# Block-sparse attention with a feed-forward network: masks and first weights moved to the front, the other weights paced over two items, V's gathered rows on another queue

## The chip, the cores and the metric

The kernel runs on one core of a Trainium2 chip. The metric is the time of one execution in microseconds (us) on the device. TensorE (PE) multiplies matrices; VectorE (DVE), ScalarE (ACT) and GpSimd (POOL) do elementwise work; SyncE (SP) here only issues DMA transfers. Every engine works through its own list of instructions in order and waits for the others by semaphores. A DMA that an engine issues stands in that engine's list like any other instruction.

## The reference

```python
# q, k, v: (4 sequences, 8 heads, 768 positions, 64); blocks of 32 positions, 24 blocks; 3 sampled blocks per query block
scores = scale * np.matmul(q, k.transpose(0, 1, 3, 2))
mask = np.abs(blk_i - blk_j) <= window                       # window = 1
mask = mask | (blk_i == 0) | (blk_j == 0) | (blk_i == n_blocks - 1) | (blk_j == n_blocks - 1)
for qb in range(n_blocks):
    for kb in sampled_blocks[qb]:
        mask[qb * block:(qb + 1) * block, kb * block:(kb + 1) * block] = True
scores = np.where(mask, scores, -1000000000.0)
attn = softmax(scores)                                       # over the keys
x = np.matmul(attn, v).transpose(0, 2, 1, 3).reshape(3072, 512)
h = x @ w_in                                                 # 512 x 2048
g = np.maximum(0.01 * h, h)
return g @ w_out                                             # 2048 x 512
```

## The kernel before

**Tiles and items.** Twelve tiles of 64 query rows make a sequence. Tile 0 holds the first and the last block, which see all 768 keys; each other tile T has 384 keys: its window, the two end blocks and six sampled blocks. A *unit* is one tile of one pair of heads, so a tile has four units (and tile 0 two parts in each). Four tiles make an *item* of 256 rows; three items make a sequence, twelve the whole. The main loop takes one unit as a step, so the first item is steps 0 to 15, the second 16 to 31, the third 32 to 47.

**Attention of a unit.** Values of 32 bits are split into two 16-bit halves so that TensorE can multiply them. `scores` (L697) multiplies the queries' halves (`qs`, and `qxs` with the halves swapped) by the gathered keys `kg`. The *score pass* `unit_ttr` (L706, on DVE) adds the mask row `em`, scales and takes the minimum; `unit_exp` (L718, ACT) takes the exponential and its sum; `pair_norm` gives `r`, the reciprocal of the sum. In the first item alone, TensorE turns the probabilities: `unit_high` (L738) builds a diagonal matrix of `r` from an identity (`eye32`), `unit_turn` (L756) multiplies by it and splits the result into `pt`. In later items ACT and DVE split the probabilities (`pp`, L745 and L766) and a DMA transposes them into `pt` (L771). `pair_av` (L798) multiplies V's rows by `pt`.

**Gathering.** `gather_k` copies a tile's keys from `kt` into one of two buffers `kg`, the sampled blocks on POOL (L640), at addresses that POOL reads from `offs`. V's halves are written to `scr` in memory (L496); `gather_v` loads a tile's rows from there into one of two buffers `vg`: the window (L659) and, when a buffer is new to a sequence, the two end blocks (L663) on SP's queue, the sampled blocks with an indirect DMA on POOL (L666).

**Masks.** `build_masks` makes `offs`, the table `mask` and `eye32`: small DVE instructions, one POOL instruction (L272) and a matmul of TensorE (L281). It is called in step 1 and set behind a score pass by `behind`, which adds an ordering edge.

**Feed-forward.** For each finished item `ffn_h` (L833) multiplies by w_in, `ffn_act1`, `ffn_max` and `ffn_act2` apply the nonlinearity and split, `ffn_o` (L860) multiplies by w_out. The weights come in four quarters. The first two items take the quarters one at a time as they get ready, later items all at once.

**Weights.** `prep_weights` is a generator. A quarter has one part of w_in and one of w_out; a part is loaded in groups of 1 MB (the last two parts in groups of 0.5 MB). The loads are issued on SP (L344); the weights come as 64-bit numbers, and each group is *decoded* to 32 bits (L351 on ACT, L352, L353 and L355 on DVE), a finished part is squared and summed (`squares`, L197 on TensorE) for its scale, and split into halves (L414 on ACT, L419 on DVE). The main loop advances the generator by credits: the table `"wr"` says from which step on how many credits a step gives. Decoding a group of 1 MB costs four.

**What sets the order.** The code gives each instruction a priority; a scheduler places them on the engines' lists. Edges added by `behind` fix an order where the code asks for it.

Of the kernel before, what the change touches and what calls it, by code (L numbers as in the profile page):

```python
# [15 lines left out]
AF = mybir.ActivationFunctionType  # L16
# [44 lines left out]
    "wlate": 1200,  # L61
    "wr": [(0, 1.8), (16, 3.5)],
    "wsplit": "dddddddd",
# [5 lines left out]
def tile_block_sparse_attention_ffn(  # L69
# [151 lines left out]
    def latest():  # L221
        return nc.cur_bb.bb.instructions[-1].name
# [140 lines left out]
    def prep_weights():  # L363
# [33 lines left out]
        behind(begin, last_sp["q"])  # L397
        yield 1
        invs = {}

# [165 lines left out]
    def prep_q(b, j, i, rq):  # L566
# [16 lines left out]
        nc.sync.dma_start_transpose(out=qs, in_=flat(qa))  # L583
        last_sp["q"] = latest()
        qxs = pa.tile([P, H, P], F16, tag="qxs", name=f"qxs_{nm}", bufs=2)
        nc.sync.dma_start(out=qxs[:D], in_=qs[D:])
        nc.sync.dma_start(out=qxs[D:], in_=qs[:D])
        qstack[b, j, i] = (qs, qxs, inv)
        yield 0.8
# [64 lines left out]
    def gather_v(b, T):  # L654
# [3 lines left out]
        t0 = (T - 1) * Q2  # L658
        nc.sync.dma_start(out=vg[:, 0, :], in_=scr[b][t0:t0 + P, :])  # L659
        if vends.get(n) != b:  # L660
            vends[n] = b
            for i, at in enumerate((0, S - BLOCK)):
                nc.sync.dma_start(  # L663
                    out=vg[Q2 + i * BLOCK:Q2 + (i + 1) * BLOCK, 2, :], in_=scr[b][at:at + BLOCK, :])
# [67 lines left out]
    def unit_high(u):  # L732
        u.r = u.pair.r[:, u.pi:u.pi + 1]
        if u.item.n < CFG["pe_t"]:
            if u.parts == 2 or u.pi == 0:
                u.pair.pp = pa.tile([P, 2, 2, KEYS], F16, tag="pp", name=f"pp_{u.nm}", bufs=CFG["pp"])
            u.diag = u.pair.pp.rearrange("p a l t -> p (a l t)").bitcast(F32)[:, u.pi * P:(u.pi + 1) * P]
            nc.gpsimd.tensor_scalar(out=u.diag, in0=eye32, scalar1=u.r, scalar2=None, op0=ALU.mult)  # L738
            return
# [320 lines left out]
    for hp in range(NP):  # L1060
        load_v(0, hp)
    begin = len(nc.cur_bb.bb.instructions)
    load_rows()
    behind(begin + 1, last_sp["k", NP - 1])
    start(("v", 0), prep_v(0))

# [48 lines left out]
    for u in units:  # L1115
        it, ui = u.item, u.k * NP + u.hp
        b, nb = it.b, it.b + 1

        if step == 1:
            begin = len(nc.cur_bb.bb.instructions)  # L1120
            build_masks()
            behind(begin, last_ttr[0])
        if step == 2:
# [32 lines left out]
        for w in CFG["ord"]:  # L1156
# [50 lines left out]
            elif w == "w":  # L1207
# [5 lines left out]
                while wcredit >= 1.0:  # L1213
                    c = next(weights, "end")
                    wcredit -= c if c != "end" else wcredit
                if step < 16:
                    behind(begin, last_ttr[0])
# [72 lines left out]
```

## Time and profile before

| | |
|---|---|
| median of three runs | 869.46 us (865.9 to 872.94) |
| the profiled execution | 867.32 us, its span 865.6 us, mean granted TensorE clock 0.963 |
| TensorE busy | 745.7 us, 86% of the span |
| VectorE busy | 601.8 us, 70% |
| ScalarE busy | 509.9 us, 59% |
| GpSimd busy | 356.3 us, 41% |
| DMA | 135.33 MB, mean 156 GB/s |

The profile is of one execution. A row of a group names the line, the engine, the operation, the output and the inputs by the program's names, and the shapes; then the count, the busy time and the mean of one in nanoseconds, and behind the second bar the idle time just before them with what ended it. A row of a stretch gives the busy time (and the number of instructions) of PE, PE's weight loads, DVE, ACT and POOL, the granted clock, the DMA engines' share and their GB/s. Durations of neighbours on one engine can overlap at their ends, so a group's busy time is less than its count times its mean.

### The profile page before, as it was taken

What the parts mean: (1) busy time and instruction counts of PE and PEld (TensorE: products, weight loads), DVE (VectorE), ACT (ScalarE), POOL (GpSimd) and SP (SyncE); (2) the same over time, 40 slices, a digit from 0 to 9 for tenths busy, and PEclk for the clock granted to TensorE, in tenths of its full rate; (3) what the DMA queues carried; (4) which work ended last, traced back from release to release, by engine and by line L of the source; (5) the groups of instructions that cost most, each with busy time, mean ns of one, the idle gap of its engine ahead of it and who ended that gap; (6) DMA issues with size and microseconds to landing.
All of it is one profiled execution on the core that took longest, in us unless ns stands there. A gap on an engine that the chain in (4) does not pass through costs nothing.

```text
span 865.6 us, 20081 instructions
## 1 busy us (share of the span) xinstructions
PE 745.7 (86%) x7140; PEld 494.9 (57%) x7140; DVE 601.8 (70%) x1595; ACT 509.9 (59%) x1183; POOL 356.3 (41%) x473
## 2 busy tenths in 40 slices
PE   1456667766998899998999989999999999999997
PEld 1245545443756565665666566666666666666674
DVE  4668998988968678757966777778667676663221
ACT  4556676775634667666656757667467566553211
POOL 0416744642125346345543554453434554532121
PEclk9968979887999999999999999999999999999999
DMA  9877489998648879898759899967678576566000
GB/s 205 162 225 237 160 191 230 234 216 181 137 104 145 172 163 211 160 170 147 194 124 177 159 162 203 199 133 183 144 131 175 116 158 148 120 139 86 26 2 25
DMA packets 312771, 135.33 MB, mean 156 GB/s; under 512 B 279773, under 2 KB 292062, under 8 KB 312670
## 3 DMA queue, kind: packets, MB, share of 16 engines
q1 hardware_dynamic: 307038, 116.74, 64.9%
q0 software_dynamic: 5632, 17.31, 8.2%
q8 instruction: 56, 0.92, 0.5%
q14 instruction: 45, 0.37, 0.1%
HBM read 65.58 MB, written 12.58 MB: 90 GB/s over the span
## 4 chain that ended last, share of the span: by engine, by line
PE 43%; DVE 20%; DMA 18%; ACT 8%; issue 5%; SPq 3%; POOL 1%; POOLq 1%; ACTq 0%; DVEq 0%
PE o L860 17%; PE h L833 17%; PE av L798 4%; PE s L697 4%; DMA kt<-k_k 3%; DVE pp L766 3%; ACT p L718 3%; DVE p L706 3%; DMA rq<-in_q_dram 3%; DMA qs_q<-qa_q 3%; DMA qxs_q<-qs_q 2%; DMA pt<-pp 2%; DMA wbuf<-in_moe_w_out_dram 2%; DVE ht L842 1%; DMA rk<-in_k_dram 1%
## 5 line engine op out<-in xcount | busy, mean ns | idle before, releaser
L860 PE MATMUL o<-W,g 128*128 128x512 f16 x1152 | 273.8, 383 | 9.3 <-DVE g L846 6.7
L833 PE MATMUL h<-x,W 128*128 128x256 f16 x2304 | 276.0, 277 | 1.9 <-ACT ht L839 1.9
L833 PEld LDWEIGHTS <-W 128*128 128x128 f16 x2304 | 223.9, 100 | 49.0 <-issue 14.2
L847 POOL TENSOR_TENSOR g<-ht,g 128x512 f16<-128x512 f32 x96 | 116.4, 1213 | 312.7 <-DVE g L846 279.1
L860 PEld LDWEIGHTS <-g 128*128 128x128 f16 x1152 | 108.2, 98 | 132.4 <-issue 15.0
L718 ACT ACTIVATE p<-p,mx 128x384 f32<-128x384 f32 x208 | 126.1, 607 | 98.0 <-DVE mx L706 66.7
L640 POOL COPY kg<-kt 128x256 f16 x264 | 133.1, 531 | 76.6 <-PE s L697 42.6
L766 DVE SCALAR_TENSOR_TENSOR pp<-p,r,pp 128x384 f16<-128x384 f32 x188 | 125.3, 694 | 33.1 <-ACT pp L745 32.4
L666 POOL DMA_INDIRECT vg<-scr,rows x88 | 94.2, 1071 | 69.5 <-PE av L798 47.4
L842 DVE SCALAR_TENSOR_TENSOR ht<-ht 128x512 f32<-128x512 f32 x96 | 67.8, 706 | 75.2 <-ACT ht L839 75.0
L706 DVE CUSTOM_DVE_ANT_0 p<-s,em,nsc 128x384 f32<-128x384 f32 x176 | 102.9, 610 | 21.9 <-PE s L697 17.3
L745 ACT ACTIVATE pp<-p,r 128x384 f16<-128x384 f32 x188 | 104.1, 604 | 17.1 <-DVE r L730 15.6
L798 PE MATMUL av<-pt,vg 128*64 128x128 f16 x2112 | 80.8, 225 | 19.7 <-DMA pt<-pp 13.6
L798 PEld LDWEIGHTS <-vg 128*64 128x64 f16 x2112 | 68.3, 112 | 49.1 <-issue 43.9
L839 ACT ACTIVATE ht<-h,gd 128x512 f32<-128x512 f32 x80 | 54.1, 677 | 63.9 <-PE h L833 51.0
L697 PE MATMUL s<-kg,qs_q 128*64 128x384 f16 x352 | 60.7, 343 | 21.5 <-DVE mx L706 21.2
L697 PE MATMUL s<-kg,qxs_q 128*64 128x384 f16 x352 | 60.0, 336 | 6.1 <-DMA qxs_q<-qs_q 6.1
L697 PEld LDWEIGHTS <-qs_q 128*64 128x64 f16 x416 | 26.9, 110 | 55.5 <-issue 43.5
L846 DVE CAST g<-ht 128x512 f16<-128x512 f32 x96 | 42.3, 441 | 10.3 <-PE o L860 8.3
L730 DVE RECIPROCAL r<-sum 128x2 f32<-128x2 f32 x96 | 15.4, 160 | 36.3 <-ACT sum L729 35.6
L718 ACT ACTIVATION_READ_ACCUMULATOR p<-p,mx 128x1 f32 x208 | 39.1, 188 | 0.0
L571 ACT ACTIVATE qa_q<-rq 128x512 f16<-128x512 f32 x25 | 15.7, 628 | 38.8 <-DMA rq<-in_q_dram 38.8
(136 smaller groups left out, 762.1 us busy)
## 6 DMA issues: line engine op xcount, KB each, us to landing
vg<-scr SPq DMA_DIRECT2D x44, 256.0 KB, 3.8
qxs_q<-qs_q SPq DMA_DIRECT2D x48, 128.0 KB, 2.6
v<-in_v_dram SPq DMA_DIRECT2D x32, 192.0 KB, 4.8
scr<-v SPq DMA_DIRECT2D x16, 384.0 KB, 4.7
W<-in_moe_w_in_dram SPq DMA_DIRECT2D x5, 1024.0 KB, 9.4
rq<-in_q_dram SPq DMA_DIRECT2D x20, 256.0 KB, 6.1
out_dram<-ob SPq DMA_DIRECT2D x20, 256.0 KB, 3.1
rk<-in_k_dram SPq DMA_DIRECT2D x24, 192.0 KB, 4.7
```

The source lines that it names most:

```text
L640: nc.gpsimd.tensor_copy(out=kg[:, :, slot * BLOCK:(slot + 1) * BLOCK], in_=kt[:, :, bass.ds(off, BLOCK)])
L666: nc.gpsimd.indirect_dma_start(out=vg[:n_, c, :], out_offset=None, in_=scr[b][:, :], in_offset=bass.IndirectOffsetOnAxis(ap=rows[:n_, c - ...
L697: nc.tensor.matmul(o, a, k, start=(n == 0), stop=(n == 1)))
L706: nc.vector.tensor_tensor_reduce(out=u.p[i], in0=u.sp[i], in1=kgs[u.b, u.T][1] if u.T else zero.to_broadcast([P, KEYS]), scale=u.nsc, scal ...
L718: nc.scalar.activation(u.p[i], u.p[i], AF.Exp, scale=-1.0, bias=u.mx[:, :1], accum_out=u.pair.sum[:, u.pi, i:i + 1])
L745: nc.scalar.activation(pp[:, 0, :], p, AF.Copy, scale=u.r)
L766: nc.vector.scalar_tensor_tensor(out=pp[:, 1, :], in0=p, scalar=u.r, in1=pp[:, 0, :], op0=ALU.mult, op1=ALU.subtract)
L798: nc.tensor.matmul(o, a, m, start=(c == 0 and l == 0), stop=(c == n - 1 and l == 1)))
L833: nc.tensor.matmul(c.ph[:, i], w, x, start=(d == 0 and m == 0), stop=(d == NP - 1 and m == 2)))
L842: nc.vector.scalar_tensor_tensor(out=c.t, in0=c.t, scalar=0.01, in1=c.t, op0=ALU.mult, op1=ALU.max)
L847: nc.gpsimd.tensor_tensor(out=c.g[:, 1], in0=c.t, in1=c.g[:, 0], op=ALU.subtract)
L860: nc.tensor.matmul(o, a, w, start=(c.first and i == 0 and m == 0), stop=(c.last and i == 1 and m == 2)))
```

## The change

Six edits:

1. `build_masks` is called ahead of the main loop, right behind the row loads, and no longer in step 1 behind a score pass.
2. The generator of the weights is advanced once more ahead of the main loop, and a new stage in it lets four groups be loaded instead of two, behind the last transpose of the first sequence's keys. The second group is ordered behind the second half of the `qxs` copies instead of the `qs` transpose.
3. From step 16 on a step gives 1.7 credits instead of 3.5, and from step 32 on 4.5. (Ahead of step 16 it stays at 1.8.)
4. For the first sequence V's window and end rows are loaded from GpSimd's queue instead of SP's.
5. The diagonal matrix is made on ScalarE instead of GpSimd.
6. In step 0 the weights' instructions are no longer ordered behind a score pass.

```diff
-    "wr": [(0, 1.8), (16, 3.5)],
+    "wr": [(0, 1.8), (16, 1.7), (32, 4.5)],
...
         load(2)
         behind(begin, last_sp["q"])
+        yield 1
+        begin = len(nc.cur_bb.bb.instructions)
+        load(4)
+        behind(begin, last_sp["k", NP - 1])
...
         nc.sync.dma_start_transpose(out=qs, in_=flat(qa))
-        last_sp["q"] = latest()
         qxs = pa.tile([P, H, P], F16, tag="qxs", name=f"qxs_{nm}", bufs=2)
         nc.sync.dma_start(out=qxs[:D], in_=qs[D:])
         nc.sync.dma_start(out=qxs[D:], in_=qs[:D])
+        last_sp["q"] = latest()
...
-        nc.sync.dma_start(out=vg[:, 0, :], in_=scr[b][t0:t0 + P, :])
+        queue = nc.sync if b else nc.gpsimd
+        queue.dma_start(out=vg[:, 0, :], in_=scr[b][t0:t0 + P, :])
...
-                nc.sync.dma_start(
+                queue.dma_start(
                     out=vg[Q2 + i * BLOCK:Q2 + (i + 1) * BLOCK, 2, :], in_=scr[b][at:at + BLOCK, :])
...
-            nc.gpsimd.tensor_scalar(out=u.diag, in0=eye32, scalar1=u.r, scalar2=None, op0=ALU.mult)
+            nc.scalar.activation(u.diag, eye32, AF.Copy, scale=u.r)
...
+    next(weights)
     begin = len(nc.cur_bb.bb.instructions)
     load_rows()
     behind(begin + 1, last_sp["k", NP - 1])
+    build_masks()
     start(("v", 0), prep_v(0))
...
-        if step == 1:
-            begin = len(nc.cur_bb.bb.instructions)
-            build_masks()
-            behind(begin, last_ttr[0])
...
-                if step < 16:
+                if 0 < step < 16:
                     behind(begin, last_ttr[0])
```

The order of the instructions on the engines moves with it. In the names below the digits behind `p`, `pp`, `s` and `pt` are the item in its sequence, the tile in the item, the pair of heads and, for score passes, the part; the last number is a buffer's. Line numbers of the changed program are a few higher than before.

ScalarE, from the first unit's exponential on, before:

```order
L718 ACTIVATE p_0_0_0_0_240,sum_0_0_0_246<-p_0_0_0_0_240,mx_0_0_0_242 128x384
L718 ACTIVATE p_0_0_0_1_241,sum_0_0_0_246<-p_0_0_0_1_241,mx_0_0_0_242 128x384
L571 ACTIVATE qa_q_0_1_262,ss_q_0_1_261<-rq_0_1_207 128x512
L571 ACTIVATE qa_q_0_1_375,ss_q_0_1_374<-rq_0_1_207 128x512
L718 ACTIVATE p_0_0_1_0_311,sum_0_0_0_246<-p_0_0_1_0_311,mx_0_0_1_313 128x384
L718 ACTIVATE p_0_0_1_1_312,sum_0_0_0_246<-p_0_0_1_1_312,mx_0_0_1_313 128x384
L476 ACTIVATE v_0_0_265,ssv_264<-v_0_209 128x768
L476 ACTIVATE v_0_0_265,ssv_264<-v_1_212 128x768
L476 ACTIVATE v_0_0_265,ssv_264<-v_2_215 128x768
L476 ACTIVATE v_0_0_265,ssv_264<-v_3_218 128x768
L645 ACTIVATE em_1_466<-mask 128x384
L645 ACTIVATE em_2_715<-mask 128x384
```

and now:

```order
L723 ACTIVATE p_0_0_0_0_281,sum_0_0_0_287<-p_0_0_0_0_281,mx_0_0_0_283 128x384
L723 ACTIVATE p_0_0_0_1_282,sum_0_0_0_287<-p_0_0_0_1_282,mx_0_0_0_283 128x384
L649 ACTIVATE em_1_466<-mask 128x384
L649 ACTIVATE em_2_715<-mask 128x384
L723 ACTIVATE p_0_0_1_0_312,sum_0_0_0_287<-p_0_0_1_0_312,mx_0_0_1_314 128x384
L723 ACTIVATE p_0_0_1_1_313,sum_0_0_0_287<-p_0_0_1_1_313,mx_0_0_1_314 128x384
L743 ACTIVATE pp_0_0_0_337<-eye_88,r_0_0_0_334 128x128
L743 ACTIVATE pp_0_0_1_358<-eye_88,r_0_0_0_334 128x128
L575 ACTIVATE qa_q_0_1_303,ss_q_0_1_302<-rq_0_1_207 128x512
L575 ACTIVATE qa_q_0_1_376,ss_q_0_1_375<-rq_0_1_207 128x512
L764 ACTIVATE pt_0_0_0_339<-turn_0_0_0_340 128x384
L480 ACTIVATE v_0_0_306,ssv_305<-v_0_209 128x768
```

The mask rows `em` and the diagonals `pp` stand ahead of the next queries' squares (`qa`), where all four of V's squares and those of the queries stood ahead of the mask rows; the diagonals were not on this engine.

SyncE, behind the load of V, before:

```order
L241 DMA rows<-in_sampled_blocks_dram 32x11x1 x6
L344 DMA W<-in_moe_w_out_dram 128x2x1024
L583 DMA_TRANSPOSE qs_q_0_1_517<-qa_q_0_1_375 128x8x128
L516 DMA rq_1_0_668<-in_q_dram 128x8x64
L496 DMA scr_564<-v_0_0_265 128x6x256
L344 DMA W<-in_moe_w_out_dram 128x2x1024
L586 DMA qxs_q_0_1_519<-qs_q_0_1_517 64x1024
L587 DMA qxs_q_0_1_519<-qs_q_0_1_517 64x1024
L496 DMA scr_564<-v_0_1_569 128x6x256
L496 DMA scr_564<-v_0_2_646 128x6x256
L496 DMA scr_564<-v_0_3_729 128x6x256
```

and now:

```order
L344 DMA W<-in_moe_w_out_dram 128x2x1024 x2
L241 DMA rows<-in_sampled_blocks_dram 32x11x1 x6
L587 DMA_TRANSPOSE qs_q_0_1_517<-qa_q_0_1_376 128x8x128
L520 DMA rq_1_0_668<-in_q_dram 128x8x64
L344 DMA W<-in_moe_w_in_dram 128x2x1024
L500 DMA scr_564<-v_0_0_306 128x6x256
L589 DMA qxs_q_0_1_519<-qs_q_0_1_517 64x1024
L590 DMA qxs_q_0_1_519<-qs_q_0_1_517 64x1024
L500 DMA scr_564<-v_0_1_569 128x6x256
L344 DMA W<-in_moe_w_out_dram 128x2x1024
L500 DMA scr_564<-v_0_2_646 128x6x256
```

Both groups of the first w_out part stand ahead of the sampled rows and the query transpose, and two more weight loads stand among the writes of V to `scr`.

VectorE, around the probability splits of the last tile of sequence one, before:

```order
L154 RECIPROCAL v_s<-v_inv 128x1
L873 TENSOR_TENSOR beta_all<-top,v_inv 128x1
L730 RECIPROCAL r_2_3_2_3760<-sum_2_3_2_3639 128x2
L492 SCALAR_TENSOR_TENSOR v_1_0_2829<-v_0_2151,v_s,v_1_0_2829 128x6x64 x2
L842 SCALAR_TENSOR_TENSOR ht_1_0_3228<-ht_1_0_3228 128x512
L766 SCALAR_TENSOR_TENSOR pp_2_3_2_3763<-p_2_3_2_0_3631,r_2_3_2_3760,pp_2_3_2_3763 128x384
L766 SCALAR_TENSOR_TENSOR pp_2_3_2_3763<-p_2_3_3_0_3671,r_2_3_2_3760,pp_2_3_2_3763 128x384
L846 CAST g_1_0_3231<-ht_1_0_3228 128x512
L881 SCALAR_TENSOR_TENSOR ob_0_0_2115<-o_0_12_0_3146,beta_3_3273,ob_0_0_2115 128x512
L492 SCALAR_TENSOR_TENSOR v_1_1_3626<-v_1_2326,v_s,v_1_1_3626 128x6x64 x2
L881 SCALAR_TENSOR_TENSOR ob_0_1_2117<-o_0_12_1_3147,beta_3_3273,ob_0_1_2117 128x512
```

and now:

```order
L771 SCALAR_TENSOR_TENSOR pp_2_3_0_3566<-p_2_3_0_0_3445,r_2_3_0_3557,pp_2_3_0_3566 128x384
L771 SCALAR_TENSOR_TENSOR pp_2_3_0_3566<-p_2_3_1_0_3487,r_2_3_0_3557,pp_2_3_0_3566 128x384
L423 SCALAR_TENSOR_TENSOR W<-W,wi_s 128x512 x3
L142 TENSOR_REDUCE v_tot<-v_sum 128x1
L423 SCALAR_TENSOR_TENSOR W<-W,wi_s 128x512
L847 SCALAR_TENSOR_TENSOR ht_1_0_3075<-ht_1_0_3075 128x512
L143 TENSOR_SCALAR v_tot<-v_tot 128x1
L771 SCALAR_TENSOR_TENSOR pp_2_3_2_3712<-p_2_3_2_0_3560,r_2_3_2_3709,pp_2_3_2_3712 128x384
L771 SCALAR_TENSOR_TENSOR pp_2_3_2_3712<-p_2_3_3_0_3620,r_2_3_2_3709,pp_2_3_2_3712 128x384
L851 CAST g_1_0_3078<-ht_1_0_3075 128x512
L147 TENSOR_SCALAR v_ex<-v_tot 128x1
L352 TENSOR_SCALAR W<-W 128x512 x3
```

Where V's splits for sequence two and the output of the last quarter stood, the splits of the last w_in part and the decodes of the last w_out part stand now.

## The prediction

> **What bounds the kernel now.** I read the busy time by stage first. The stages are cut where VectorE starts the first score pass (L706) of a tile: 60.6 us is the first tile of the sampled kind, 165.6 us the first tile of the third item, 214.7 us the last tile of sequence one, 318.6 us the fifth tile of sequence two.
>
> ```profile
> core 0: us, PE busy (x) PEld busy (x) DVE busy (x) ACT busy (x) POOL busy (x), PEclk, DMA share, GB/s
> 0.00:27.00 27.00, 4.63 (x18) 3.07 (x19) 9.19 (x39) 10.79 (x17) 0.82 (x6) 1.00 1.06 216
> 27.00:60.60 33.60, 16.00 (x119) 12.14 (x119) 23.92 (x89) 18.74 (x42) 11.18 (x19) 0.85 0.80 195
> 60.60:165.60 105.00, 74.19 (x805) 55.85 (x804) 97.38 (x233) 72.68 (x159) 58.12 (x72) 0.87 0.80 206
> 165.60:214.70 49.10, 31.94 (x305) 18.34 (x303) 42.83 (x115) 35.26 (x84) 19.23 (x23) 0.86 0.98 201
> 214.70:318.60 103.90, 94.93 (x883) 63.06 (x882) 78.69 (x217) 59.76 (x137) 35.06 (x50) 0.99 0.73 149
> 318.60:865.60 547.00, 524.02 (x5019) 342.44 (x5016) 349.80 (x907) 312.68 (x746) 231.89 (x305) 0.99 0.69 139
> ```
>
> The same windows for L706 alone confirm the cuts: each pass is two instructions (the pass and the read of its minimum), a tile of this kind has four, so 56 rows are seven tiles, 24 are three, 48 are the last tile, the first tile of sequence two (eight passes) and three more.
>
> ```profile
> 60.60:165.60 105.00, 17.14 (x56) 0.87 0.80 206
> 165.60:214.70 49.10, 7.15 (x24) 0.86 0.98 201
> 214.70:318.60 103.90, 14.26 (x48) 0.99 0.73 149
> ```
>
> VectorE (DVE) is the bound from 60.6 to 165.6 us (idle 7.6 of 105.0 us) and nearly so to 214.7 us (idle 6.3). From there TensorE (PE) is: idle 9.0 of 103.9 us, then 23.0 of 547.0. The first 60.6 us are bound by neither: DVE idle 17.8 + 9.7, PE idle 22.4 + 17.6. So a gain can come only from idle time ahead of 60.6 us and from moving work between a stretch where DVE is full and one where it is not.
>
> The timeline shows what the first 60 us wait for, engine by engine (start, length, and in brackets the idle time before it).
>
> ```profile
> 26.49 0.62 DVE L706 CUSTOM_DVE_ANT_0 p<-s,zero,nsc 128x384 f32<-128x384 f32 x1 [7.14 <-PE s L697]
> 29.53 1.21 POOL L640 COPY kg<-kt 128x256 f16 x3 [12.18 <-DVE hit L266]
> 36.73 0.15 DVE L730 RECIPROCAL r<-sum 128x2 f32<-128x2 f32 x1
> 37.43 0.43 POOL L272 TENSOR_SCALAR_AFFINE_SELECT at<-ok 24x66 f32<-24x66 f32 x1
> 37.86 1.19 POOL L738 TENSOR_SCALAR pp<-eye,r 128x128 f32<-128x128 f32 x2
> 37.91 1.06 PE L281 MATMUL mask_ps<-at,tmps 24*128 24x33 f32 x4 [5.93 <-POOL at L272]
> 39.77 2.91 PE L756 MATMUL turn<-pp,p 128*128 128x128 f32 x12
> 60.67 0.62 DVE L706 CUSTOM_DVE_ANT_0 p<-s,em,nsc 128x384 f32<-128x384 f32 x1 [2.45 <-PE turn L756]
> ```
>
> The masks are computed after the first pass; TensorE, stuck in order at the mask's matmul, turns nothing until 39.77 us, though r is there at 36.73. Behind that, ScalarE (ACT) waits in order for a query load that it does not need yet, and DVE for ACT; and from 37.5 to 46.5 us the DMA engines move 6 GB/s at a share of 0.12.
>
> ```profile
> ACT qa_q L571 <- DMA rq<-in_q_dram: 6.5, 2, 5.7
> DVE v L492 <- ACT v L489: 4.3, 2, 3.7
> 37.50:46.50 9.00, 7.76 (x40) 6.33 (x41) 6.80 (x24) 7.58 (x16) 1.90 (x4) 1.00 0.12 6
> ```
>
> **The change part by part.** Prices of single instructions:
>
> ```profile
> L738 POOL TENSOR_SCALAR pp<-eye,r 128x128 f32<-128x128 f32 x16 | 12.5, 788 | 17.4 <-DVE r L730 17.3
> L729 ACT ACTIVATE sum<-sum,floor 128x2 f32<-128x2 f32 x88 | 25.1, 286 | 0.7
> L805 ACT ACTIVATE avt<-av 128x256 f32<-128x256 f32 x48 | 17.7, 368 | 16.3 <-PE av L798 16.0
> L492 DVE SCALAR_TENSOR_TENSOR v<-v,v_s,v 128x384 f16<-128x384 f32 x32 | 21.9, 724 | 6.0 <-ACT v L489 6.0
> L353 DVE SCALAR_TENSOR_TENSOR W<-W 128x1024 int32<-128x1024 int32 x9 | 11.3, 1258 | 0.0
> L355 DVE SCALAR_TENSOR_TENSOR W<-W 128x1024 int32<-128x1024 int32 x9 | 11.1, 1230 | 0.0
> L352 DVE TENSOR_SCALAR W<-W 128x1024 int32<-128x1024 int32 x12 | 8.7, 723 | 3.5 <-ACT W L351 3.5
> L353 DVE SCALAR_TENSOR_TENSOR W<-wbuf,W 128x512 int32<-128x512 int32 x8 | 6.2, 790 | 0.0
> L355 DVE SCALAR_TENSOR_TENSOR W<-wbuf,W 128x512 int32<-128x512 int32 x8 | 5.3, 683 | 0.0
> L352 DVE TENSOR_SCALAR W<-W 128x512 int32<-128x512 int32 x8 | 3.9, 499 | 0.9 <-ACT W L351 0.9
> L419 DVE SCALAR_TENSOR_TENSOR W<-W,wi_s 128x1024 f16<-128x1024 f32 x6 | 7.9, 1322 | 0.0
> L554 DVE SCALAR_TENSOR_TENSOR k_k<-rk,k_s,k_k 128x768 f16<-128x768 f32 x12 | 12.1, 1011 | 2.4 <-ACT k_k L552 2.4
> L766 DVE SCALAR_TENSOR_TENSOR pp<-p,r,pp 128x384 f16<-128x384 f32 x188 | 125.3, 694 | 33.1 <-ACT pp L745 32.4
> L666 POOL DMA_INDIRECT vg<-scr,rows x22: 899/1062/1943, 62.9 to 208.2; - x22
> L659 SPq DMA_DIRECT2D vg<-scr x12: 338/368/572, 62.0 to 261.8; - x12
> ```
>
> *Masks and the first decode early; the diagonal on ScalarE.* The mask arithmetic and one weight decode (0.72 + 1.26 + 1.23 = 3.2 us) now stand ahead of the first pass, inside DVE's 7.14 us wait at 26.49; that pass keeps its time, and about 5 us of DVE work (the decode and some 2 us of small mask rows) leave the 10.2 us between it and r. So r comes at about 31.5 instead of 36.73. The diagonal takes two instructions on ACT, priced between 0.286 and 0.368 us; I take 0.33, nearer the wider row, so sixteen cost ACT 5.3 us (4.6 to 5.9), covered by ACT's 32 us of idle time from 60.6 to 165.6; were half of it bare, it would cost 2.6. The turn then starts at about 32.5, where it was 39.77.
>
> From the turn to the first sampled pass lie 20.9 us. Eight V splits (L492, 8 x 0.72 = 5.8 us) now stand behind that pass, and DVE's longest wait on ACT (3.7 us) goes, since the next item's query squares move behind it on ACT: 20.9 - 5.8 - 3.7 = 11.4, so 44. I allow 2.5 for the longer work now ahead of it on ACT: **46.5 instead of 60.7**. Of the 14.2 us, 5.8 are work that is still owed, so **8.4 us of idle time are saved**; bounds 3 (a query load that still lands late) to 11.
>
> *Weights in items one and two (1.8 a step kept, then 1.7 for 3.5).* Counting both orders on DVE up to the third item's first pass, the new one lacks one decode of the large form (3.2), three of the half form but for one L355 (3 x 0.50 + 3 x 0.79 + 2 x 0.68 = 5.2), two splits of W (2.6) and small rows (1.7), and has a K split (1.0), two probability splits (1.4) and scale rows (1.0) more: 9.3 us less. Neighbours overlap at their ends, so I count 8.6 us. DVE is full there, so this comes off the time. All in all the third item starts 8.4 + 8.6 = 17 us earlier.
>
> *Two megabytes of w_out ahead of the query transpose on SP.* They are queued at about 35 us and fall into those 9 us; a third load now stands ahead of the first V write, a fourth ahead of the third. At the 201 to 206 GB/s of the stages a 1 MB load takes 5 us; what V's write loses, the earlier split must give back. I allow **4 us** of new waits (0 to 10) before the third item: the net gain there is 13.
>
> *V's rows on GpSimd.* Eleven tiles' rows and four ends leave SP for POOL. Where SP took 0.37 us for one, POOL takes about what an indirect one takes: 15 x 1.06 = 16 us (5.5 to 29), for 12.5 us of diagonals that left, against 46.9 us that POOL idles from 60.6 to 165.6. The first tile has five issues before its V is whole where it had two: 3 us later, hidden because TensorE's V product of that tile now stands behind the scores of the tile two on. At 0 in the sum. [...]
>
> *The third item gives part back (4.5 a step).* For TensorE the unit prices are
>
> ```profile
> 188.63 2.64 PE h L833 x24
> 415.65 2.59 PE o L860 x12
> 315.69 0.86 PE L798 MATMUL av<-pt,vg 128*64 128x128 f16 x24 [0.94 <-DVE xf L808]
> 173.89 10.34 DMA pt<-pp
> ```
>
> From 165.6 to the last tile's first pass DVE has another 22.6 - 9.3 = 13.3 us less (weights, and FFN that waits for them); overlap off, 12.4: that stage is 36.7 instead of 49.1 us. What was not done then comes in the next stage: by the order TensorE has two blocks of h (2 x 2.64), 24 matmuls of o (24 x 0.216), 72 of av (3 x 0.86) and 28 of the weights' squares (at one to two av matmuls each, 1 to 2 us) more: 15 us. That stage is TensorE's: 94.9 + 15 + 9.0 idle = 119 instead of 103.9. DVE, with 78.7 + 21, stays below. Net **+2.7**.
>
> *After 318.6 us* both orders have done the same on DVE and TensorE, and ACT has only the sixteen diagonals behind it: 547.0 us unchanged.
>
> **Sum.** 8.4 + 8.6 - 4 - 2.7 = 10.3 us off the span of 865.6 us: 855.3. The profiled execution took 867.3 us, 1.7 us outside its span, and lies 2.1 below the median of 869.46; I take the 10.3 us off the median: **859 us**.
>
> **The rivals.**
> *More than that, 848 us:* no new waits (4), the sampled pass at 44 (2.5), and in the third item DVE loses the waits that fill its 6.3 us of idle time, as the 10.34 us of a probability transpose in the chain at 173.89. For it: the DMA share of 0.98 there is made of weights that now load sooner. Against: the half-size loads still go there, at 4.5 a step.
>
> *GpSimd's queue takes it back, 867 us:* at 1.94 us each the ten issues for the first two tiles take 19 us where POOL had six of four indirect ones; tile one's V comes 8 us late (half of the 13 more, and the two ends), and TensorE, in order, stands at its product with DVE behind it: 859 + 8. Against: POOL idles nearly half that stage. [...]
>
> *The weights ahead of V on SP, 868 us:* two extra megabytes stand in front of the last V write, 10 us at 201 GB/s. If the first product of a sampled tile is due before V's rows, the 10 show but for the 1 us by which the order puts that product later: 859 + 9. Against: the 9 us at 6 GB/s, which hold 1.8 MB.
>
> *Slower, 880 us:* the last quarter decides. Its eight half-size loads and decodes now stand around the last tile, in order on DVE in front of V's splits for sequence two, and on TensorE its squares stand ahead of the scale of sequence two's first query. If a load comes behind a probability transpose of 10.34 us, everything of sequence two stands behind it; two such waits cost 21 us: 859 + 21. It decides where the loads of the third item (some 3 MB beside 3 MB of K and V and the transposes) need more than the stage's 36.7 us. For it: the DMA share of 0.98 in that stage before. Against: 0.73 in the next one, into which half of it falls.
>
> **How the numbers follow.** Forecast 859 (own range 853 to 864) 0.43; 848 0.17; 867 0.12; 868 0.13; 880 0.15. About 1% (8.7 us: 860.8 and 878.2) is what a measurement of this kernel can tell from no change. Faster by that: all of the 0.17, and three quarters of the forecast's own range lie below 860.8, 0.33: 0.50. Slower: 0.12 of the 880 case. The rest, 0.38, is within. The range 845 to 876 leaves out 0.14 of the 880 case and 0.04 below the 848.
>
> **What would show it.** In the changed profile: the first pass that reads em at 46.5 us (44 to 50) instead of 60.67, and the turn near 32.5; the third item's first pass near 153; the last tile of sequence one near 189; the fifth tile of sequence two near 308; 547 us from there. The forecast is wrong if the third item starts after 160, if GpSimd's direct issues take well over 1.1 us with TensorE waiting for vg, or if DVE waits at L352 for a load of the last quarter while TensorE stands at a wo square.

## The result, and the profile after

| | before | changed |
|---|---|---|
| median | 865.37 us (20 runs, 859.0 to 872.94) | 862.85 us (20 runs, 855.7 to 867.16) |
| ratio | 1 | 0.9947, 95% interval 0.9925 to 0.9968 |
| profiled execution | 867.32 us, span 865.6 | 863.27 us, span 861.6 |
| mean granted clock of the profiled execution | 0.963 | 0.948 |

The ratio is worth 4.6 us (2.8 to 6.5), in the profiled pair 4.0 us; the two medians lie 2.5 us apart. Ratios and median clocks, here and below, leave out the few runs that took over 1.5% more than the fastest of their kernel. The forecast was a gain of 10.3 us. That the 859 us forecast lies so near 862.85 is luck in part: it was taken off a median of 869.46, and more runs of the kernel before have one of 865.37, from which the same gain would have given 855.

The windows of the changed kernel, cut at the same passes as before (now L711): the first tile of the sampled kind, the first tile of the third item, the last tile of sequence one, the fifth tile of sequence two.

```profile
core 0: us, PE busy (x) PEld busy (x) DVE busy (x) ACT busy (x) POOL busy (x), PEclk, DMA share, GB/s
0.00:44.00 44.00, 18.57 (x90) 13.00 (x91) 28.80 (x120) 26.92 (x58) 6.60 (x19) 0.98 0.99 228
44.00:151.00 107.00, 74.65 (x768) 54.70 (x769) 94.20 (x230) 75.69 (x174) 53.18 (x71) 0.75 0.87 201
151.00:186.70 35.70, 25.10 (x246) 15.58 (x240) 33.95 (x84) 28.11 (x68) 15.49 (x20) 0.86 1.06 253
186.70:309.10 122.40, 109.87 (x1024) 72.32 (x1022) 98.33 (x260) 69.23 (x154) 45.13 (x58) 0.96 0.74 152
309.10:861.60 552.50, 525.34 (x5029) 344.13 (x5026) 342.80 (x907) 312.47 (x746) 233.11 (x305) 0.99 0.69 138
```

| start of | before | forecast | changed | gain |
|---|---|---|---|---|
| first sampled pass | 60.6 | 46.5 | 44.0 | 16.6 |
| third item | 165.6 | 153 | 151.0 | 14.6 |
| last tile of sequence one | 214.7 | 189 | 186.7 | 28.0 |
| fifth tile of sequence two | 318.6 | 308 | 309.1 | 9.5 |
| end of span | 865.6 | 855.3 | 861.6 | 4.0 |

So each stage of the forecast is found within 2.5 us down to 309 us, and then 5.5 us are lost in a stretch that was to stay as it was. But VectorE's passes are not TensorE's time, and in that region TensorE is the bound (busy 525.3 of 552.5 us). The timelines of TensorE have the first scores of the fifth tile of sequence two, of the kernel before and of the changed one:

```profile
313.91 0.35 PE L697 MATMUL s<-kg,qs_q 128*64 128x384 f16 x2
```

```profile
306.62 0.35 PE L702 MATMUL s<-kg,qs_q 128*64 128x384 f16 x2
```

On TensorE the gain there is 7.3 us; VectorE's pass merely follows sooner (2.5 us behind instead of 4.7). So 3 us of the 10.3 are missing at this point and 3.3 more at the end.

The timeline of the changed kernel's early part: r, the diagonal on ScalarE, the turn, and the first sampled pass.

```profile
29.12 0.16 DVE L735 RECIPROCAL r<-sum 128x2 f32<-128x2 f32 x1
29.37 0.69 ACT L743 ACTIVATE pp<-eye,r 128x128 f32<-128x128 f32 x2 [1.00 <-DVE r L735]
44.00 0.62 DVE L711 CUSTOM_DVE_ANT_0 p<-s,em,nsc 128x384 f32<-128x384 f32 x1 [0.83 <-PE turn L761]
```

And the groups of the changed kernel for what was moved: V's rows on GpSimd, the indirect gathers, the diagonal on ScalarE.

```profile
L664 POOL DMA_DIRECT2D vg<-scr x11 | 6.8, 614 | 52.0 <-PE av L803 41.3 <-DMA scr<-v 10.6
L668 POOL DMA_DIRECT2D vg<-scr x4 | 2.1, 541 | 0.0
L671 POOL DMA_INDIRECT vg<-scr,rows x88 | 93.9, 1067 | 46.7 <-issue 18.3 <-PE av L803 12.1 <-DMA scr<-v 11.7
L743 ACT ACTIVATE pp<-eye,r 128x128 f32<-128x128 f32 x16 | 5.5, 392 | 1.5 <-DVE r L735 1.0 <-DVE W L352 0.4
```

**TensorE works longer for the same matmuls.** Its busy time was 745.7 us; the five rows above add up to 753.5, for 7140 matmuls in both. The difference is the clock: by the mean granted clock, (1 - 0.963) x 865.6 x 2 = 64 us at half speed before and (1 - 0.948) x 861.6 x 2 = 90 us after. Both figures leave out the start. The clock's records begin at 43.5 us before and at 35.5 us in the changed kernel, and the profile counts the time ahead of them as full speed (the 1.00 in the first rows); but the score matmuls there take 0.53 us, as at 45.17 us of the changed kernel at a clock of 0.50, and 0.33 to 0.35 behind at 1.00 (a turn of six matmuls 1.65 us at 33.68 us and 0.94 at 35.83). With the whole start counted at half speed, an estimate from these times, it is 108 us before and 124 after. TensorE is busy for 60 and 79 us of these, and half of the 19 us between is 9, by that estimate about the 7.8 by which its busy time grew.

In both traces the clock is recorded as 0.50 or 1.00. The changed kernel from 93.56 us on, cut every 3.41 us (columns as above; the last three are the clock, the DMA share and GB/s):

```profile
93.56:96.98 3.42, 3.42 (x34) 2.96 (x33) 3.42 (x8) 1.92 (x6) 3.42 (x5) 0.50 0.20 71
96.98:100.39 3.41, 0.98 (x10) 0.50 (x9) 3.41 (x15) 2.86 (x6) 1.24 (x2) 1.00 0.01 2
100.39:103.80 3.41, 1.50 (x26) 1.30 (x24) 3.41 (x7) 3.01 (x7) 1.73 (x2) 0.50 0.19 23
103.80:107.21 3.41, 1.15 (x7) 0.54 (x7) 3.41 (x10) 1.58 (x3) 1.83 (x2) 0.50 1.01 214
107.21:110.63 3.42, 2.00 (x29) 1.31 (x26) 3.27 (x5) 3.31 (x8) 2.73 (x3) 0.50 1.13 199
110.63:114.04 3.41, 3.41 (x18) 2.27 (x17) 3.41 (x10) 2.04 (x5) 2.07 (x4) 0.50 0.61 125
114.04:117.45 3.41, 3.41 (x33) 3.04 (x31) 2.16 (x6) 2.98 (x9) 0.00 (x0) 1.00 1.24 191
```

TensorE is busy 0.98 us of one such window, and the clock of the next is 0.50; it is 1.00 again behind a window in which TensorE is busy throughout (3.41 us). Behind the start, and but for one at the very end, the 24 stretches at half clock in the two traces last 3.4, 6.8, 10.2, 13.7 or 17.1 us, all whole multiples of 3.41 us. In these two traces each of the 19 windows of that length at full clock in which TensorE was busy for less than 1.4 us was followed by half clock, and none with more than 2.0 us was; back at full it was only behind windows with 2.7 us or more. Among 35 runs of the kernel before the granted clock lies at a median of 0.955, among the 20 of the changed one at 0.946. In the 23 runs that the first experiments had of the kernel before, each per cent of clock goes with 4.3 us of time; in the 28 and the 34 of the two later sets it is 3.0 and 2.6 us.

### The profile page after: what moved, and what is told of

Its sections match the earlier page's. It is cut to its first block, busy times and chain, and to the rows that moved or that the text cites. A ratio compares the mean times of both kernels' runs of the same rounds, so it can differ in the third digit from the quotient of the medians.

```text
span 861.6 us, 20081 instructions
## 1 busy us (share of the span) xinstructions
PE 753.5 (87%) x7140; PEld 499.7 (58%) x7140; DVE 598.1 (69%) x1595; ACT 512.4 (59%) x1199; POOL 353.5 (41%) x472
## 4 chain that ended last, share of the span: by engine, by line
PE 52%; DMA 19%; DVE 16%; ACT 6%; issue 4%; SPq 2%; POOLq 0%; POOL 0%; ACTq 0%; DVEq 0%
PE h L838 20%; PE o L865 19%; PE av L803 5%; DMA qs_q<-qa_q 5%; PE s L702 5%; DMA pt<-pp 4%; DVE pp L771 3%; DMA qxs_q<-qs_q 3%; DMA kt<-k_k 3%; DVE p L711 2%; ACT p L723 2%; DMA wbuf<-in_moe_w_out_dram 2%; DVE W L353 2%; DMA v<-in_v_dram 1%; PE turn L761 1%
## 5 line engine op out<-in xcount | busy, mean ns | idle before, releaser
L711 DVE CUSTOM_DVE_ANT_0 p<-s,em,nsc 128x384 f32<-128x384 f32 x176 | 102.5, 610 | 24.8 <-PE s L702 20.2
L671 POOL DMA_INDIRECT vg<-scr,rows x88 | 93.9, 1067 | 46.7 <-issue 18.3
L803 PE MATMUL av<-pt,vg 128*64 128x128 f16 x2112 | 83.0, 229 | 17.5 <-DVE top L448 7.8
L803 PEld LDWEIGHTS <-vg 128*64 128x64 f16 x2112 | 70.4, 115 | 46.2 <-issue 39.5
L702 PE MATMUL s<-kg,qs_q 128*64 128x384 f16 x352 | 62.6, 348 | 23.8 <-DVE mx L711 20.7
```

The source lines that it names most:

```text
L671: nc.gpsimd.indirect_dma_start(out=vg[:n_, c, :], out_offset=None, in_=scr[b][:, :], in_offset=bass.IndirectOffsetOnAxis(ap=rows[:n_, c - ...
L702: nc.tensor.matmul(o, a, k, start=(n == 0), stop=(n == 1)))
L711: nc.vector.tensor_tensor_reduce(out=u.p[i], in0=u.sp[i], in1=kgs[u.b, u.T][1] if u.T else zero.to_broadcast([P, KEYS]), scale=u.nsc, scal ...
L803: nc.tensor.matmul(o, a, m, start=(c == 0 and l == 0), stop=(c == n - 1 and l == 1)))
```

## The experiments

All ratios are to the kernel before on the same chip; 0.001 is 0.87 us. One thing holds for every kernel here: the scheduler places the instructions anew, so a run that undoes one part also has another order. Between the changed kernel and the one that only moves V's rows back to SyncE, the lists of TensorE's 7140 matmuls in order of time show 600 lines of difference.

| kernel | ratio (95%) | median clock |
|---|---|---|
| changed | 0.9947 (0.9925 to 0.9968) | 0.946 |
| old rate, the rest changed | 0.9922 (0.9892 to 0.9953) | 0.950 |
| new rate alone | 1.0077 (1.0041 to 1.0112) | 0.944 |
| rate 1.8, 2.5, 4.5 | 1.0086 (1.0052 to 1.0121) | 0.938 |
| rate 1.8, 5.0 | 1.0019 (0.9983 to 1.0054) | 0.944 |
| rate 2.5, 3.5 | 0.9956 (0.9925 to 0.9988) | 0.949 |
| V's rows on SyncE | 1.0041 (1.0008 to 1.0074) | 0.941 |
| the same, without 2 MB ahead | 1.0005 (0.9981 to 1.0030) | 0.943 |
| diagonal on GpSimd | 1.0101 (1.0064 to 1.0137) | 0.943 |
| both of these undone | 1.0032 (1.0001 to 1.0063) | 0.949 |
| masks late | 1.0015 (0.9981 to 1.0049) | 0.946 |
| two extra pairs | 1.0119 (1.0068 to 1.0170) | 0.948 |
| four extra pairs | 1.0098 (1.0057 to 1.0139) | 0.958 |

### The rate of the weights

*The old rate in the changed kernel.*

```diff
-    "wr": [(0, 1.8), (16, 1.7), (32, 4.5)],
+    "wr": [(0, 1.8), (16, 3.5)],
```

> The changed kernel with the weights' old rate (1.8 a step, from step 16 on 3.5); masks, V's rows and the diagonal stay as changed. Theory one, the last quarter: what is missing from the forecast went where the last quarter now stands, at 4.5 a step around the last tile of sequence one. Then the third item starts some 8 us later than in the changed kernel (TensorE's first scores near 158 instead of 150.0 us), but the stage from the last tile of sequence one to the fifth tile of sequence two falls from 126 to some 110 us, the fifth tile starts at 302 to 305 instead of 306.6, and the time is 2 to 5 us under the changed kernel's. Rival, the clock: TensorE's 7.8 us of extra busy time for the same matmuls come from the early work being packed differently, whichever rate is used; then TensorE's busy time up to the fifth tile stays above 222 us (218.3 before, 226.1 changed) and the time stays within 2 us of the changed kernel's. The prediction's own sum: the rate is worth 8.6 - 2.7 and about 4 of new waits, so undoing it costs some 2 us.

0.9922: 2 us under the changed kernel by the two ratios, though their intervals overlap. Its windows at the same cuts:

```profile
42.70:161.10 118.40, 82.18 (x813) 59.10 (x813) 104.98 (x244) 80.03 (x179) 54.28 (x72) 0.78 0.82 203
161.10:212.10 51.00, 35.59 (x359) 22.69 (x358) 44.50 (x117) 34.45 (x82) 23.48 (x28) 0.83 0.92 188
212.10:310.60 98.50, 90.58 (x843) 59.75 (x842) 78.63 (x213) 59.46 (x137) 35.12 (x50) 0.98 0.81 156
```

This pair differs by the rate alone, and shows it as a loan. With the new rate the stretch to the third item is 11.4 us shorter and the third item 15.3 us (51.0 to 35.7), for VectorE has 10.8 and 10.6 us less to do. But TensorE also does 7.5 and 10.5 us less there, and 19.3 us more in the next stretch, which is its own: that one is 23.9 us longer (98.5 to 122.4). Of 26.7 us, 23.9 are paid back by the fifth tile of sequence two. The first theory's place is right, but its gain of 2 to 5 us is not shown by the ratio's interval, and the fifth tile does not start earlier (its first scores at 309.5 us, not 302 to 305). The clock rival's sign holds: TensorE is busy 224.7 us up to there, above 222, so in the changed kernel the longer matmuls are there at either rate.

*The new rate alone*, with all else as before:

```diff
-    "wr": [(0, 1.8), (16, 3.5)],
+    "wr": [(0, 1.8), (16, 1.7), (32, 4.5)],
```

> The kernel before with the new rate of the weights alone (1.8 a step, from step 16 on 1.7, from step 32 on 4.5); no other part of the change. The prediction's sum for the rate: 8.6 us less VectorE work ahead of the third item, 2.7 given back, so some 2 to 6 us faster than before. What undoing the rate in the changed kernel showed speaks for no gain: there the time fell by some 2 us (859.5) rather than rising, so the rate alone should be 0 to 3 us slower than before. If the halved clock comes from the rate, the mean clock falls from 0.958 to below 0.950; if it comes from the early start, it stays at 0.955 to 0.965.

1.0077, so 6.7 us (3.6 to 9.7) slower than before, worse than either expectation, with the clock at 0.944. Its windows:

```profile
58.90:165.90 107.00, 74.74 (x712) 52.07 (x712) 89.34 (x221) 71.54 (x161) 55.28 (x72) 0.76 0.81 190
165.90:203.90 38.00, 27.45 (x299) 17.65 (x299) 35.00 (x93) 28.34 (x66) 12.72 (x18) 0.82 1.03 251
203.90:320.40 116.50, 107.30 (x991) 71.62 (x987) 95.33 (x251) 67.87 (x152) 41.33 (x54) 0.97 0.71 146
```

VectorE has 8.0 us less to do ahead of the third item (97.38 to 89.34; the forecast said 8.6), and the stretch is 2 us longer: VectorE now idles 17.7 of 107.0 us, where it idled 7.6 of 105.0, and the granted clock there is 0.76 instead of 0.87.

*Three other rates.* Each is the changed kernel with another table.

```diff
-    "wr": [(0, 1.8), (16, 1.7), (32, 4.5)],
+    "wr": [(0, 1.8), (16, 2.5), (32, 4.5)],
```

> The changed kernel with a rate between the two: 1.8 a step, from step 16 on 2.5, from step 32 on 4.5. If the lower rate beside the second and third item is what costs TensorE its clock (mean clock 0.944 for the new rate alone against 0.956 for the kernel before, and 6.6 us slower), a rate between gives a ratio between those of the new rate (0.9947) and the old (0.9922), and a clock between 0.946 and 0.950. If the optimum lies between, as a balance of VectorE's load before the third item and the work given back after it would have it, the ratio is 0.987 to 0.991.

```diff
-    "wr": [(0, 1.8), (16, 1.7), (32, 4.5)],
+    "wr": [(0, 1.8), (16, 5.0)],
```

> The changed kernel with the weights faster than ever: 1.8 a step, from step 16 on 5.0. By the clock theory TensorE gets its FFN work sooner, its windows without work become fewer, the mean clock rises over 0.950, and the time is that of the old rate or up to 3 us less (ratio 0.988 to 0.993). By VectorE's load, which the prediction's sum rests on, the decodes now crowd the second item even more: the third item starts 5 to 8 us later than the 161.1 us of the old rate and the ratio is 0.996 to 1.003.

```diff
-    "wr": [(0, 1.8), (16, 1.7), (32, 4.5)],
+    "wr": [(0, 2.5), (16, 3.5)],
```

> The changed kernel with the old rate behind step 16 (3.5) and a faster one ahead of it (2.5 instead of 1.8). By VectorE's load: the sampled tiles of item one lose what the second item gains, ratio 0.991 to 0.995, as the old rate's. By the clock theory: more weights are ready at the second item, TensorE's FFN work starts earlier, the mean clock is over 0.950 and the ratio below 0.990. If the two megabytes ahead are then too few, VectorE waits at a decode for a load and the ratio is above 0.997.

1.0086, 1.0019 and 0.9956. The rate between is the worst of all, 12 us above its neighbour on the one side and 14 above that on the other; no curve runs through these points. Its twelve runs spread from 868.3 to 879.9 us, and the profiled one took 877.03. The time of the fast rate came out as VectorE's load has it, but not by its way: its third item starts at 184.3 us, 23 and not 5 to 8 later than with the old rate. Its clock of 0.944 is below what the clock theory expected, and so is that of the last rate (0.949), whose ratio lies between its expected ranges. What cost the rate between its time stands in TensorE's waits from 150 to 225 us, around its third item (engine and line, what it waited for, us in total, times, longest):

```profile
PE av L803 <- DMA pt<-pp: 18.1, 3, 9.1
PE k_sum L131 <- ACT k_k L544: 9.1, 1, 9.1
```

```profile
152.80:210.60 57.80, 32.66 (x338) 20.54 (x336) 46.70 (x117) 37.02 (x86) 20.02 (x26) 0.74 1.03 208
```

Its third item takes 57.8 us where the changed kernel's takes 35.7, with TensorE at the V product for probability transposes while half-size weight loads stand between them on SyncE. That looks like the way of the slower rival (880 us), met in a neighbour of the changed kernel, whose median is 877.07 us beside 867.04 of the kernel before. In the changed kernel, from 150 to 225 us, the second takes 0.6 us and the first is not among the seven longest.

### V's rows and the diagonal

*V's rows on SyncE again.*

```diff
-        queue = nc.sync if b else nc.gpsimd
+        queue = nc.sync
```

> The changed kernel with V's rows of sequence one issued by SyncE again; all else as changed. The prediction's own sum: moving them was worth nothing, so within 1 us of the changed kernel. [...] The weights ahead of V: with the rows back on SyncE's queue they stand behind two extra megabytes of w_out, V of the first sampled tile comes up to 10 us later, and the time is 2 to 9 us above the changed kernel's.

1.0041, 8 us above the changed kernel: not within 1 us, but the size of the case of the weights ahead of V. TensorE's waits do not show the way that case was told, though: for the indirect rows of V it waits 1.7 us in all from 20 to 160 us (3.1 in the changed kernel, the faster one), for the direct ones not at all.

*The same, without the two megabytes ahead.*

```diff
         behind(begin, last_sp["q"])
         yield 1
-        begin = len(nc.cur_bb.bb.instructions)
-        load(4)
-        behind(begin, last_sp["k", NP - 1])
         yield 1
```

> V's rows of sequence one on SyncE again, and besides the two megabytes of w_out no longer queued ahead of the third query's transpose (they come when their decode is due); masks, diagonal and rate as changed. With the rows on SyncE and the two megabytes ahead, the kernel measured some 8 us over the changed one (1.0041 of the kernel before against 0.9947). Theory, the weights ahead of V: those rows lost because the two megabytes stand in front of them, so without these the loss goes and the time is 858 to 864 on a scale where the kernel before is 866 (a ratio of 0.991 to 0.998). Rival, the place of the rows: they cost on SyncE whatever is ahead of them, since they stand among the probability transposes; then the ratio stays at 1.002 or more.

1.0005, between the two bounds: by the ratios 3 of the 8 us go with the megabytes and 5 stay, but its interval overlaps that of the run before. Undecided; both may have a part, or the new order has.

*The diagonal on GpSimd again*, V's rows staying there:

```diff
-            nc.scalar.activation(u.diag, eye32, AF.Copy, scale=u.r)
+            nc.gpsimd.tensor_scalar(out=u.diag, in0=eye32, scalar1=u.r, scalar2=None, op0=ALU.mult)
```

> The changed kernel with the diagonal for sequence one's first tiles built on GpSimd again (0.79 us each before) instead of ScalarE. The prediction priced the sixteen on ScalarE as hidden, so it made nothing of this part by itself: within 1 us. Theory, the parts need each other: on GpSimd the diagonal now stands in order behind the five issues of V's rows and the indirect ones (1.07 us each); a turn then waits up to 5 us for it, the eight tiles of items one and two lose 1 to 2 us each, the third item starts at 155 to 165 instead of 150.0 us, and the time is 3 to 10 us above the changed kernel's.

1.0101, 13 us above the changed kernel and more than the 3 to 10 expected; the third item starts at 162.2 us, within the 155 to 165. The groups of this kernel by form show the turn, and the diagonal:

```profile
L761 PE MATMUL turn<-pp,p 128*128 128x128 f32 x120 | 25.7, 377 | 20.1 <-POOL pp L743 12.8 <-DVE pt L765 5.5 <-DVE q_inv L153 0.9
L743 POOL TENSOR_SCALAR pp<-eye,r 128x128 f32<-128x128 f32 x16 | 16.1, 1013 | 14.9 <-DVE r L735 12.3 <-DVE q_ex L147 2.6
```

TensorE waits 12.8 us for the diagonal, and one takes GpSimd 1.01 us on average where ScalarE takes 0.39 (and where it took 0.79 before). A few long ones make these averages: the middle one of the sixteen takes 0.67 us here and 0.60 before, the longest 2.5 and 2.4.

*Both undone.*

```diff
-        queue = nc.sync if b else nc.gpsimd
+        queue = nc.sync
...
-            nc.scalar.activation(u.diag, eye32, AF.Copy, scale=u.r)
+            nc.gpsimd.tensor_scalar(out=u.diag, in0=eye32, scalar1=u.r, scalar2=None, op0=ALU.mult)
```

> The changed kernel with both undone that were undone singly: V's rows of sequence one on SyncE again and the diagonal on GpSimd again; masks and rate as changed. Theory, the two parts need each other: the 12 us that the diagonal cost on GpSimd came from its standing behind V's rows in GpSimd's order (TensorE's turn waited 12.8 us for it, up to 4.8 at once), so without those rows the diagonal costs little and the time is that of the run with V's rows alone back on SyncE, 868 to 873. Rival, each costs for itself: the two losses (about 7 and 12 us) add up, 880 to 886.

1.0032: as with V's rows alone on SyncE, and not the sum of both losses. Its groups:

```profile
L761 PE MATMUL turn<-pp,p 128*128 128x128 f32 x120 | 25.8, 380 | 13.7 <-POOL pp L743 7.6 <-DVE pt L765 5.4 <-POOL kg L644 0.7
L743 POOL TENSOR_SCALAR pp<-eye,r 128x128 f32<-128x128 f32 x16 | 15.5, 974 | 20.2 <-DVE r L735 20.2
```

So the losses are not additive: the diagonal's place costs 13 us when V's rows are on GpSimd and nothing that can be measured when they are not, though TensorE waits for it there too. The pair of edits together is worth 7 us (1.0032 against 0.9947).

### Masks late

```diff
-    build_masks()
     start(("v", 0), prep_v(0))
...
+        if step == 1:
+            begin = len(nc.cur_bb.bb.instructions)
+            build_masks()
+            behind(begin, last_ttr[0])
         if step == 2:
```

> The changed kernel with the masks built behind the first score pass again, as before; all else as changed. The prediction's sum gives the early masks (with the first decode moved ahead of the first pass) 8.4 us of saved idle time ahead of the first sampled tile: then the second tile's scores start at 44 to 48 instead of 36.7 us, the third item some 8 us later than 150.0, and the time is 5 to 8 us above the changed kernel's. Theory, lost anyway: what is saved early is eaten later, since VectorE and TensorE give the time back between 180 and 310 us; then the fifth tile of sequence two comes within 2 us of the changed kernel's 306.6 us and the time does too.

1.0015, so 6 us above the changed kernel, within the expectation. But not by its way: the first sampled pass of the profiled execution starts at 45.4 us and the third item at 152.7, 1.4 and 1.7 us later than in the changed kernel; the diagonals on ScalarE and the first decode stay early there. r comes at 29.38 us, 0.26 later than with the masks early: the mask arithmetic now fills VectorE's wait behind the first passes. In this profile the other theory's sign holds instead, with the first scores of the fifth tile of sequence two at 307.4 us, 0.8 later than in the changed kernel. But that execution, 864.12 us, was one of the quicker ones of its kernel (median 868.56). Where its 6 us go, the profile doesn't show.

### More matmuls for the clock

The score pair of a unit is issued two (or four) times more into its bank ahead of the real ones, in sequence one; the results are overwritten.

```diff
+        if us[0].b == 0:
+            emits = [lambda hh=hh: nc.tensor.matmul(
+                sp[hh * D:(hh + 1) * D, :], st[:, h, c0:c0 + Q2], keys, start=True, stop=True)
+                for _ in range(2) for hh in range(2)] + emits
         together(emits)
```

> The changed kernel with more matmuls and nothing else: ahead of the scores of each of sequence one's units, the last half's first-term score matmul pair is issued twice more into the same score bank, which the real scores then overwrite; about 0.17 us a pair at the full clock, so 48 units x 2 x 0.17 = 16 us of TensorE work that computes nothing kept. The clock theory (in the changed kernel 1 - 0.948 of 861.6 us, so about 90 us at the halved clock against 64 before, and 7.8 us more busy time for the same matmuls; among the runs of the kernel before, each per cent of mean clock goes with 4.3 us): more activity keeps the clock up, the mean clock over the run rises to 0.955 or more, and the time stays the same or falls by up to 4 us although TensorE has more to do. Rival, the clock only mirrors the waits: the time rises by some of the 16 us, 3 to 12, since every unit's scores come 0.35 us later.

> As the run with two extra pairs a unit, but with four: 32 us of TensorE work at the full clock that computes nothing kept. The clock theory: the mean clock rises further, to 0.965 or more, the busy time of sequence one's real matmuls falls, and the third item starts within 3 us of 150.0; the time is within 4 us of the changed kernel's. Rival, the clock only mirrors the waits: 6 to 24 us above the changed kernel's.

The code makes 26 score groups of these units, not 48, so the extra work is 26 x 2 x 0.17 = 9 us, and 18 us with four pairs (an estimate: at full clock the changed kernel's pairs start 0.16 to 0.19 us apart, as at 37.48 and 37.64 us). The times are 1.0119 and 1.0098, 15 and 13 us above the changed kernel. With two pairs the clock hardly moves (0.948). With four it does rise (0.958, though not to the 0.965 of the clock theory), and TensorE's busy time of 761.8 us is 8 above the changed kernel's instead of 18, so the real matmuls became some 10 us cheaper. It buys no time: the third item starts at 159.4 us instead of 151.0, and VectorE waits longer for TensorE. From 44 to 160 us its longest waits are, with four pairs,

```profile
DVE p L715 <- PE turn L765: 8.1, 3, 7.1
```

and in the changed kernel

```profile
DVE p L711 <- PE turn L761: 4.4, 4, 2.5
```

The rival's time held for four pairs, and with two the loss was above its 3 to 12 us. So filling the waits with work in TensorE's own order costs more here than the clock gives. That the halved clock only mirrors the waits is not shown: the real matmuls did become cheaper.

## Why the prediction was right and wrong

**Right in its times, only in part in its cause: the early part.** r at 29.12 us (forecast 31.5), the turn behind it at 29.82 (32.5), the first sampled pass at 44.0 (46.5). VectorE's longest wait on ScalarE for V's split, 3.7 us before, is 0.7 now. But the first pass did not keep its time, as the prediction had it: it starts at 23.03 us instead of 26.49. The second half of edit 2 put the second group of weights behind the `qxs` copies on SyncE, and the prediction gave that no term. The scores that wait for the copies start 5 us sooner; before and now:

```profile
25.93 0.85 PE L697 MATMUL s<-kt,qxs_q 128*64 128x384 f16 x4 [6.07 <-DMA qxs_q<-qs_q]
```

```profile
20.84 0.85 PE L702 MATMUL s<-kt,qxs_q 128*64 128x384 f16 x4 [3.29 <-DMA qxs_q<-qs_q]
```

In the kernel with the rate alone, whose copies stand where they stood before, these scores start at 23.76 us; in seven profiled kernels with the copies ahead, between 20.46 and 22.06. The early masks, to which the prediction gave the gain together with the first decode and the diagonal, are not what carries it: undoing them moves the first sampled pass by 1.4 us, undoing the diagonal by 1.1. No run undoes the order of the copies or the early decode, so how the rest divides is open.

**Right: up to the third item.** VectorE's busy time ahead of it fell from 130.5 to 123.0 us, 7.5 where the overlap-corrected forecast was 8.6; its idle time in that stretch rose from 7.6 to 12.8, 5.2 where 4 was allowed for new waits. The idle time saved ahead of the first sampled pass was 12.3 us (27.5 before, 15.2 now), where the forecast was 8.4 with an upper bound of 11. The net, 12.3 + 7.5 - 5.2, was 14.6, forecast 13: the errors in part cancel.

**Mis-sized: "the third item gives part back, 2.7".** The third item took 35.7 us (forecast 36.7). The next stretch took 122.4 (119): TensorE's busy time in it is 109.9, as forecast, but it idles 12.5 us instead of 9.0. Against the kernel before the two stretches give back 18.5 - 13.4 = 5.1 us; against the kernel that differs in the rate alone, 23.9 - 15.3 = 8.6. The idle time was taken over from a stage that no longer was the same. That the busy time comes out as forecast is luck in part: TensorE is busy 9.3 us at half clock there, 2.9 before, so some 3 of the added 15 us are the clock, for which the sum had no term. The added work is some 12, with 19 more matmuls of h in the stage instead of 48; the 24 of o and the 72 of av came as counted.

**Failed: "8.6 us of VectorE work come off the time, since VectorE is full there".** Within the changed kernel the stretch does shrink with the new rate (11.4 us for 10.8 us less work), but the gain is paid back by the fifth tile of sequence two. With the new rate alone 8.0 us left VectorE and the stretch did not shrink. So at 93% busy VectorE was not alone the bound in the kernel before. That it is one part of a loop with ScalarE and TensorE, whose granted clock there was 0.76 with the new rate alone (0.87 before), is argued from the idle time and the clock of that stretch, not shown by a run of its own. The rate, forecast at 8.6 - 2.7 = 5.9 us of gain before new waits, is worth nothing here (2 us of loss, not significant) and a loss of 6.7 us by itself.

**Failed: "V's rows on GpSimd at 0", and the diagonal "hidden, 0".** The GpSimd price was high (15 issues took 6.8 + 2.1 = 8.9 us, not 16) and the ScalarE price low (0.39 us each, not 0.33); neither matters. What was missing is that the two edits hang together: undoing them both costs 7 us, and undoing the second alone 13. By which wait V's rows gain on GpSimd stays open. So it was luck that the total came out on the right side: a gain counted at nothing stood in for one that wasn't there.

**Failed: "547.0 us unchanged" after the fifth tile.** It was 552.5, 3.3 us longer by TensorE's rows, at nearly the same busy time (524.0 and 525.3). From sequence three on TensorE's program order is the same but for about a hundred of some 7,900 matmuls and weight loads. The other eleven profiled kernels without extra matmuls, the one before among them, took between 544.2 and 558.7 us for this stretch, so one profile can't tell 3 us there from chance. This part of the shortfall stays open; so does how much of the 7.8 us that TensorE's busy time grew adds to the time.

**The rivals.** GpSimd's queue did not take it back (867): undoing it lost time, the direct issues took 0.61 and 0.54 us, and L671 kept its mean of 1.07 us. Where the landing shows, a tile's rows land 4.3 us behind their issue (median; 4.0 from SyncE before), and the end rows 6.2 us behind theirs, where it was 2.9; why is not shown. The 1.94 us an issue of that rival are the slowest of the 22 indirect issues that the prediction lists; that every issue takes them was the author's assumption, and no run shows it: the longest direct one took 0.80 us. The weights ahead of V on SyncE (868) did not occur; with the rows back there the loss is of its size, but its mechanism is not shown. The slower case (880) did not occur, but one step away, at a rate of 2.5, its waits did.

## What to carry to other kernels

Work that is postponed out of a stretch in which one engine is busy is a loan: look in the next stretch at the engine that bounds it, and price what arrives there at that engine's full time plus new waits. A busy share of 93% did not make VectorE the bound here: compare a run that takes the work away and leaves all else. Look for a small ordering edit that hides in a large one, and give it a term. Where a scheduler orders the program, an edit of one number moves hundreds of instructions, and neighbouring rates here lie up to 14 us apart, so the value of a part must be read from several neighbours and not from one.

## What was not expected of the hardware

The granted clock of TensorE falls in the middle of the kernel, again and again: 65 us at half speed behind the start before, 89 after, in stretches that are whole multiples of 3.41 us. The profile's mean clock leaves out the first 35 to 44 us, in which the score matmuls took 0.53 us, as they did later at a clock of 0.50, and not the 0.33 to 0.35 of full clock. With four extra pairs of matmuls a unit the clock was higher (0.958 instead of 0.946) and the kernel 13 us slower. Building the same 128 x 128 diagonal took GpSimd 0.60 us in the kernel before and 0.66 to 0.67 in the two kernels with the masks early (medians; single ones took up to 2.5 us), 0.39 on ScalarE.
